# Six wider token blocks instead of eight in the first network of an attention and mixture-of-experts kernel

## The chip, the cores and the metric

The kernel runs on one core of one Trainium2 chip. The metric is the device time of one execution in microseconds. A core has TensorE (PE, the matrix multiplies; PEld is its weight load, which overlaps), VectorE (DVE), ScalarE (ACT), GpSimd (POOL) and SyncE (SP, which here only issues DMAs; ACT issues some too). Each engine executes its instructions in a fixed order and stops at the first whose inputs or buffers are not ready.

## The reference

The inputs are q, k, v (4 batches, 8 heads, 576 positions, 64 wide), the weights of a first gated network and those of a second, expert network. All products are done to nearly float32 precision.

```
scores = q @ k^T / 8, masked      # heads 0-3: the last 32 positions; heads 4-7: every 4th of the last 128
x   = softmax(scores) @ v                             # 2304 tokens x 512
xn  = x / sqrt(mean(x*x) + 1e-6) * rms_g
y   = (silu(xn @ w_gate) * (xn @ w_val)) @ w_out      # first network: 512 -> 1536 -> 512, weights in float64
P   = exp(y @ gate2 - max); 8 rounds of row and column normalisation, P *= 2304/8 in each
out = sum over 8 experts of P[:, e] * (relu(y @ w1[e]) @ w2[e])     # 512 -> 1024 -> 512
```

## The kernel before

Every value that a matrix multiply reads is split into a high and a low part of TensorE's reduced float32 format (tiles of `[128, 2, 512]`, slot 0 high, slot 1 low), and each product is done in three passes (high x high, high x low, low x high).

**Attention** goes by 20 tiles, five for each batch (four of 128 tokens and one of 64). A tile (`att_tile`, L148) is a chain: 32 or 16 small multiplies into `psS`; on DVE the mask is added into `sf` (tile `sc`), then maximum and subtraction (L191 to L200); Exp on ACT (L203); sums on DVE; four transposes into `psT` and a copy to `pt` (L219); the multiplies with v into `psX`; the division into `xf` (tile `xs`, L255); two Squares on ACT with a sum (L271); two small multiplies into `psR`; a power on POOL (L282); scaling on DVE (L284); four transposes into `psXT`; and the split into the columns of `xn` (L299, L300). The first five tiles use three sets of buffers (`Set`, L91): set 0 has its own K and V buffers `kbd` and `vbd`, sets 1 and 2 borrow six slots each of the weight pool `wx`. Tiles 5 to 19 all use set 0 in "rows" mode, one after the other: K and Q of the next tile are fetched by ACT's queue after the copy to `pt`, V after the Squares. `pt` and `xs` share one buffer (tag `px`), `q` and `sc` have one each, `psS` and `psX` share one pair of PSUM banks.

**First network.** The tokens are cut into eight blocks, per batch one of 256 (two tiles) and one of 320 (three tiles). For a block, 12 calls of `gemm_h` (L437) do 12 multiplies each into `pg` and `pv` (L447), as wide as the block, and then Silu on ACT, the product on DVE and the split of `h` on ACT and POOL. After each chunk of four such calls, `gemm_out` (L411) does 4 x 12 multiplies into `po` (L421) and adds them to `partial`; the last chunk writes `partial` to DRAM (`x2d`). A block thus takes 432 multiplies. Blocks 0 and 1 go chunk by chunk while the weights come in. From block 2 on, the attention of block i+1 is written ahead of the multiplies of block i, and a planner that simulates the engines fixes each engine's order, with the program's order as priority. `xn` has two buffers, one for even and one for odd blocks; `h` has five, `hf` two.

**Weights.** The 36 weight tiles of 128 x 512 float64 numbers are numbered in the order of their use. `split_double` (L314) takes each in two halves of 256 columns. A half takes an absolute value on ACT (L344), three operations on DVE (L345, L347, L350), a scaling on ACT (L354), an addition on POOL (L355), the high part on ACT for even numbers (L358) or on POOL for odd (L360), and the low part on DVE for the gate and value weights (L366) or POOL for the output weights (L364). Numbers 0 to 25 are loaded whole into a slot of `wx`, 26 to 35 by halves into a staging pool. The scratch `m` is one of three buffers of 256 columns for numbers below 12, and half a slot of `wx` from 12 to 25.

**Gate and second network.** `gate` (L517) reads 384 tokens of `x2d` at a time, six times in all, beside the multiplies of blocks 2 to 7 and the start of the second network. Towards the end of block 7, `tail` (L691) prepares the first inputs and weights of the second network (`x_load`, `x_split`, `moe2_weights`), whose tiles reuse the slots of the first network's weights as these come free. The second network's multiplies (L803, 384 columns; L860, 512 columns) fill the rest of the time.

Of the kernel before, what the change touches and what calls it, by code (L numbers as in the profile page):

```python
# [8 lines left out]
F32 = mybir.dt.float32  # L9
# [15 lines left out]
NEG = -1.0e30  # L25

# [6 lines left out]
def attention_moe_kernel(  # L33
# [57 lines left out]
    class Set:  # L91

        def __init__(self, first=None):
            self.work = None
            self.rows = False
            if first is None:
                self.q = None
                k = apool.tile([P, 2, 832], F32, name="kbd")  # L100
                self.k = [k[:, :, :320], k[:, :, 320:]]
                self.kload = [k]
                v = apool.tile([P, 2, 1024], F32, name="vbd")
                self.v = [v[:, :, :512], v[:, :, 512:]]
# [14 lines left out]
        def load_qk(self, n, queue=None):  # L119
            queue = queue or nc.sync  # L120
            b, t = divmod(n, 5)
            if self.work is None:
                self.q = apool.tile([P, 512], F32, tag="q", name=f"q_{n}", bufs=1)
            queue.dma_start(self.q, qt[b, t])
            for hh in range(2):
                c0 = 0
                for k in self.kload:
                    c1 = c0 + k.shape[2]
                    queue.dma_start(k[64 * hh : 64 * hh + 64, hh, :], kt_[b, t, hh, :, c0:c1])
                    c0 = c1  # L130

        def load_v(self, n, queue=None):
# [3 lines left out]
            for hh in range(2):  # L136
                for i, v in enumerate(self.vload):
                    queue.dma_start(v[64 * hh : 64 * hh + 64, hh, :], vt[b, t, hh, :, c * i : c * i + c])
# [9 lines left out]
    def att_tile(n, xn, c0, bufs, after_qk=None, after_pv=None):  # L148
# [14 lines left out]
        for hp in range(4):  # L163
            for g in range(4):
                off = hp * 160 + 32 * g if hp < 2 else ((hp - 2) * 4 + g) * 64
                if rows:
                    for s in range(2):
# [4 lines left out]
                            rhs=bufs.k[hp // 2][half, s, off : off + 64],  # L172
# [42 lines left out]
        if bufs.work is None:  # L215
            pt = apool.tile([P, 512], F32, tag="px", name=f"pt_{n}", bufs=1)
# [10 lines left out]
        for hp in range(4):  # L227
            vals = bufs.v[hp // 2].rearrange("p s (a g d) -> p s a g d", a=2, g=4)
            for g in range(4):
                if rows:  # L230
                    for s in range(2):
# [4 lines left out]
                            rhs=vals[half, s, hp % 2, g, :],  # L236
# [13 lines left out]
        if bufs.work is None:  # L250
            xf = apool.tile([P, 512], F32, tag="px", name=f"xs_{n}", bufs=1)
# [62 lines left out]
    def split_double(pool, src, name, gk, number, hi_eng, lo_eng):  # L314
# [701 lines left out]
```

## Time and profile before

| | us |
|---|---|
| three timed runs | 2147.39, 2156.18, 2156.72 |
| their median | 2156.18 |
| the profiled execution | 2151.64 |
| span of its trace, first to last instruction | 2149.9 |
| TensorE busy in the span | 2078.1 (97%) |
| VectorE, ScalarE, GpSimd busy | 1227.3, 893.7, 781.2 |

The profiled execution is 1.7 us longer than its span, and lies between the timed runs, 4.5 us under their median. A busy share is a mean over the whole span; the first 200 us, the next 390, the change to the second network (590 to 750) and the second network itself have different limits.

### The profile page before, as it was taken

To read this page: it belongs to the slowest core of one execution; us is meant where nothing else is said; L and a number is where in the kernel's file an instruction comes from. 1 tells how busy PE (TensorE), PEld (TensorE's weight loads), DVE (VectorE), ACT (ScalarE), POOL (GpSimd) and SP (SyncE) were. 2 spreads that over 40 slices of the span, in tenths; PEclk is the share of its full clock that TensorE was granted. 3 is DMA by queue.
4 is the path that set the end of the run, shared out by engine and by line. 5 is a ranking of instruction groups with operands and counts; after the bars stand their busy time and mean duration, and the time that the engine had idled before them with its cause. 6 is when DMAs were issued, how large, how long until landed. Compare 5 with 4: busy or idle time off the path is not lost.

```text
span 2149.9 us, 34621 instructions
## 1 busy us (share of the span) xinstructions
PE 2078.1 (97%) x13506; PEld 1900.2 (88%) x13506; DVE 1227.3 (57%) x2122; ACT 893.7 (42%) x1916; POOL 781.2 (36%) x853
## 2 busy tenths in 40 slices
PE   5788999999999999999999999999999999999999
PEld 4778999999988889899899988989998898999897
DVE  7987333324166756566655655665656466566553
ACT  5554443334245334434434443443344444334431
POOL 3765221212255424333413433433333333333420
PEclk7899999999999999999999999999999999999999
DMA  9323322212132212112212221221222122122110
GB/s 273 119 77 97 84 71 56 69 29 74 43 118 84 69 59 79 57 62 79 74 54 89 79 59 60 79 78 51 69 89 79 50 78 79 54 65 79 60 39 35
DMA packets 83397, 161.04 MB, mean 75 GB/s; under 512 B 10528, under 2 KB 18336, under 8 KB 83232
## 3 DMA queue, kind: packets, MB, share of 16 engines
q1 hardware_dynamic: 76128, 140.63, 21.4%
q10 hardware_dynamic: 7104, 18.19, 3.0%
q8 instruction: 106, 1.74, 0.3%
q14 instruction: 59, 0.48, 0.1%
HBM read 149.34 MB, written 9.44 MB: 74 GB/s over the span
## 4 chain that ended last, share of the span: by engine, by line
PE 85%; DVE 5%; ACT 3%; DMA 2%; POOL 2%; issue 2%; SPq 1%; ACTq 0%; POOLq 0%; DVEq 0%
PE py L860 36%; PE pa L803 18%; PE pb L803 9%; PE po L421 6%; PE pv L447 5%; PE pg L447 5%; PE pc L803 5%; DMA kbd<-in_kt 1%; PE psX L233 0%; PE psS L169 0%; DVE m_o L350 0%; DMA sd_g<-in_w_gate 0%; DMA vbd<-in_vt 0%; DVE m_o L345 0%; DMA st_w<-in_w 0%
## 5 line engine op out<-in xcount | busy, mean ns | idle before, releaser
L860 PE MATMUL py<-w,h 128*128 128x512 f32 x3456 | 860.9, 393 | 0.6 <-DVE acc L881 0.6
L860 PEld LDWEIGHTS py<-w,h 128*128 128x128 f32 x3456 | 644.0, 188 | 118.3 <-DVE acc L881 1.0
L597 POOL TENSOR_TENSOR w<-st_w,w 128x512 fp32r<-128x512 f32 x184 | 241.8, 1333 | 351.0 <-ACT w L596 343.8
L881 DVE SCALAR_TENSOR_TENSOR acc<-py,Pm,acc 128x512 f32<-128x512 f32 x264 | 194.3, 748 | 275.9 <-PE py L860 275.7
L803 PE MATMUL pa<-x_b,w 128*128 128x384 f32 x1152 | 254.3, 337 | 7.4 <-ACT w L579 6.5
L566 POOL TENSOR_TENSOR w1s<-w1r 128x256 f32<-128x256 f32 x92 | 75.0, 816 | 500.0 <-DVE w L580 499.0
L803 PE MATMUL pa<-x_t,w 128*128 128x384 f32 x1152 | 244.8, 337 | 0.0
L803 PEld LDWEIGHTS pa<-x_b,w 128*128 128x128 f32 x1152 | 207.1, 188 | 18.9 <-ACT w L579 7.7
L803 PEld LDWEIGHTS pa<-x_t,w 128*128 128x128 f32 x1152 | 206.9, 188 | 14.3 <-ACT pq L832 0.2
L447 PE MATMUL pv<-xn,w_v 128*128 128x320 f32 (+1 forms) x1152 | 185.1, 305 | 15.8 <-ACT hf L459 6.3
L421 PE MATMUL po<-h,w_o 128*128 128x320 f32 (+1 forms) x1152 | 179.3, 301 | 9.5 <-DVE partial L432 3.3
L596 ACT CAST w<-st_w 128x512 fp32r<-128x512 f32 x184 | 108.6, 621 | 190.9 <-PE pa L803 85.5
L447 PE MATMUL pg<-xn,w_g 128*128 128x320 f32 (+1 forms) x1152 | 182.6, 300 | 3.3 <-DVE hf L460 2.1
L447 PEld LDWEIGHTS pv<-xn,w_v 128*128 128x128 f32 x1152 | 165.6, 194 | 20.6 <-ACT hf L459 7.3
L421 PEld LDWEIGHTS po<-h,w_o 128*128 128x128 f32 x1152 | 161.9, 191 | 13.7 <-DVE partial L432 4.0
L447 PEld LDWEIGHTS pg<-xn,w_g 128*128 128x128 f32 x1152 | 164.1, 191 | 6.7 <-DVE hf L460 2.7
L462 POOL TENSOR_TENSOR h<-hf,h 128x256 fp32r<-128x256 f32 (+1 forms) x96 | 80.1, 837 | 218.1 <-ACT h L461 218.1
L580 DVE TENSOR_TENSOR w<-w1s,w 128x512 fp32r<-128x512 f32 x184 | 125.1, 705 | 22.0 <-ACT w L579 19.6
L580 DVE TENSOR_TENSOR w<-w1r,w 128x512 fp32r<-128x512 f32 x92 | 110.1, 1196 | 40.0 <-ACT w L579 39.4
L579 ACT CAST w<-w1s 128x512 fp32r<-128x512 f32 x184 | 110.9, 619 | 52.1 <-PE pc L803 17.0
L815 ACT ACTIVATE h<-pq 128x384 fp32r<-128x384 f32 x96 | 50.3, 524 | 185.6 <-DVE pq L844 185.5
L803 PE MATMUL pb<-x_t,w 128*128 128x384 f32 x576 | 125.2, 336 | 0.0
(160 smaller groups left out, 2697.3 us busy)
## 6 DMA issues: line engine op xcount, KB each, us to landing
st_w<-in_w SPq DMA_DIRECT2D x184, 256.0 KB, 2.8
w1r<-in_w SPq DMA_DIRECT2D x184, 256.0 KB, 2.9
vbd<-in_vt ACTq DMA_DIRECT2D x30, 256.0 KB, 4.0
kbd<-in_kt ACTq DMA_DIRECT2D x30, 208.0 KB, 3.5
sd_g<-in_w_gate SPq DMA_DIRECT2D x10, 512.0 KB, 6.9
sx<-x2d SPq DMA_DIRECT2D x24, 192.0 KB, 2.6
xr<-x2d SPq DMA_DIRECT2D x12, 384.0 KB, 3.7
out<-acc SPq DMA_DIRECT2D x18, 256.0 KB, 2.3
```

What stands on the lines that cost most here:

```text
L421: nc.tensor.matmul(po[:, :n], lhsT=ow[f][:, a, dc * P : dc * P + P], rhs=hs[blk, f][:, bb, :n], start=k == 0, stop=k == 11,)
L447: nc.tensor.matmul(ps[:, :n], lhsT=w[kt, fg][:, a, fo * P : fo * P + P], rhs=xn[:, kt, bb, :n], start=k == 0, stop=k == 11,)
L462: nc.gpsimd.tensor_tensor(out=h[:, 1, :n], in0=hf, in1=h[:, 0, :n].bitcast(F32), op=ALU.subtract)
L566: nc.gpsimd.tensor_tensor(out=s1, in0=a21, in1=a22f, op=ALU.add)
L579: nc.scalar.copy(hi, src)
L580: nc.vector.tensor_tensor(out=lo, in0=src, in1=hi.bitcast(F32), op=ALU.subtract)
L596: nc.scalar.copy(w[:, 0, :], st)
L597: nc.gpsimd.tensor_tensor(out=w[:, 1, :], in0=st, in1=w[:, 0, :].bitcast(F32), op=ALU.subtract)
L803: nc.tensor.matmul(ps[:, :TH], lhsT=w1s[ch, a, kt][:, s, q * P : q * P + P], rhs=xc[b, kt][:, t, :TH], start=first and k == 0, stop=k == 5 ...
L815: nc.scalar.activation(h[:, 0, :], src, AF.Relu)
L860: nc.tensor.matmul(ps, lhsT=hh[u, f, th][:, a, jj * P : jj * P + P], rhs=w2s[ch, f][:, bb, :], start=k == 0, stop=k == 11,)
L881: nc.vector.scalar_tensor_tensor(out=acc[j], in0=ps, scalar=Pm[:, tt, e : e + 1], in1=acc[j], op0=ALU.mult, op1=ALU.add)
```

## The change

Blocks become 256, 320, 384, 448, 448 and 448 tokens (2, 3, 3, 4, 4 and 4 tiles). `xn`, `h` and `hf` are sized for 448; `hf` has one buffer instead of two; `partial` has one buffer of 576 columns, whose two parts hold blocks 0 and 1. The gate reads 512, 384, 512, 384 and 512 tokens instead of six times 384. Set 0 borrows six slots of the weight pool `wr`; a new set `setn`, for tiles 5 to 19, has K and V buffers of half the size (the two heads on the two halves of the partitions, without a zero half). In it `pt` takes the buffer of `q`, and `xs` that of `sc`; K of the next tile is fetched after the copy to `pt`, Q and V after the Squares. Weights 4 to 31 are split 512 columns at a time, weights 0 to 31 are loaded whole and have their scratch in weight-pool slots, and 32 to 35 take staging and scratch from the same three staging buffers.

```diff
+BLK = 448
         def __init__(self, first=None):
-            self.rows = False
+            self.rows = first is None
             if first is None:
-                k = apool.tile([P, 2, 832], F32, name="kbd")
+                k = apool.tile([P, 832], F32, name="kall").unsqueeze(1)
...
-                v = apool.tile([P, 2, 1024], F32, name="vbd")
+                v = apool.tile([P, 1024], F32, name="vall").unsqueeze(1)
...
             else:
-                slots = [wx.tile([P, 2, 512], F32R, tag="w", name=f"first_{first}_{i}").bitcast(F32) for i in range(6)]
+                pool = wr if first == 0 else wx
+                slots = [pool.tile([P, 2, 512], F32R, tag="w", name=f"first_{first}_{i}").bitcast(F32) for i in range(6)]
...
+        def load_qv(self, n, queue):
+            self.load_q(n, queue)
+            self.load_v(n, queue)
...
-            pt = apool.tile([P, 512], F32, tag="px", name=f"pt_{n}", bufs=1)
+            pt = apool.tile([P, 512], F32, tag="q", name=f"pt_{n}", bufs=1)
...
-            xf = apool.tile([P, 512], F32, tag="px", name=f"xs_{n}", bufs=1)
+            xf = apool.tile([P, 512], F32, tag="sc", name=f"xs_{n}", bufs=1)
...
-        wide = number < 26
+        wide = number < 32
...
-            if number >= 12:
-                if number % 2 == 0:
-                    m_slot.append(wx.tile([P, 2, 512], F32R, tag="w", name=f"m_{name}").bitcast(F32))
-                scratch = m_slot[-1][:, number % 2, :].rearrange("p (j n) -> p j n", j=2)
-        for j in range(2):
-            cols = slice(256 * j, 256 * j + 256)
+            if number % 2 == 0:
+                m_pool = wr if number < 4 else wx
+                m_slot.append(m_pool.tile([P, 2, 512], F32R, tag="w", name=f"m_{name}").bitcast(F32))
+            scratch = m_slot[-1][:, number % 2, :]
+        step = 512 if wide and number >= 4 else 256
+        for j in range(0, 512, step):
+            cols = slice(j, j + step)
             if wide:
-                words = raw[:, 512 * j : 512 * j + 512]
+                words = raw[:, 2 * j : 2 * j + 2 * step]
             else:
-                pool_st, bufs = (stg, 3) if (2 * number + j) % 4 < 3 else (apool, 1)
-                words = pool_st.tile([P, 512], U32, tag="st", name=f"sd_{name}_{j}", bufs=bufs)
+                words = stg.tile([P, 512], U32, tag="st", name=f"sd_{name}_{j}", bufs=3)
...
-                mf = apool.tile([P, 256], F32, tag="m", name=f"m_{name}_{j}", bufs=3)
+                mf = stg.tile([P, 512], F32, tag="st", name=f"m_{name}_{j}", bufs=3)[:, :step]
...
-            partials[blk] = mpool.tile([P, 4, n], F32, tag=f"partial{blk % 2}", name=f"partial_{blk}", bufs=1)
+            if blk == 0:
+                both = mpool.tile([P, 4, 576], F32, tag="partial", name="partial_0", bufs=1)
+                partials[0], partials[1] = both[:, :, :256], both[:, :, 256:]
+            elif blk > 1:
+                partials[blk] = mpool.tile([P, 4, 576], F32, tag="partial", name=f"partial_{blk}", bufs=1)[:, :, :n]
...
-        hf = mpool.tile([P, 320], F32, tag="hf", name=f"hf_{blk}_{f}", bufs=2)[:, :n]
+        hf = mpool.tile([P, BLK], F32, tag="hf", name=f"hf_{blk}_{f}", bufs=1)[:, :n]
...
+    GATES = (0, 512, 896, 1408, 1792, NT)
...
-    for b in range(B):
-        blocks.append((b * S, 256, [(5 * b, 0), (5 * b + 1, 128)]))
-        blocks.append((b * S + 256, 320, [(5 * b + 2, 0), (5 * b + 3, 128), (5 * b + 4, 256)]))
+    for t0, t1 in ((0, 2), (2, 5), (5, 8), (8, 12), (12, 16), (16, 20)):
+        tok0 = starts[t0]
+        blocks.append((tok0, starts[t1] - tok0, [(t, starts[t] - tok0) for t in range(t0, t1)]))
...
             yield from att_tile(
-                tn, xns[i], c0, set0,
-                (lambda: set0.load_qk(tn + 1, nc.scalar)) if more else None,
-                (lambda: set0.load_v(tn + 1, nc.scalar)) if more else None,
+                tn, xns[i], c0, setn,
+                (lambda: setn.load_k(tn + 1, nc.scalar)) if more else None,
+                (lambda: setn.load_qv(tn + 1, nc.scalar)) if more else None,
...
-    ready = {2: (0,), 3: (1,), 4: (2,), 6: (3,)}
-    for i in range(2, 8):
-        if i < 7:
+    for i in range(2, 6):
+        if i < 5:
             run(block_att(i + 1))
-            spread(moe1_chunks([(i, 0), (i, 1), (i, 2)]), 34, [(later(g), 34) for g in ready.get(i, ())])
+            spread(moe1_chunks([(i, 0), (i, 1), (i, 2)]), 34, [(later(i - 2), 34)])
         else:
-            spread(moe1_chunks([(i, 0), (i, 1), (i, 2)]), 34, [(tail(), 34), (later(4), 34)])
+            spread(moe1_chunks([(i, 0), (i, 1), (i, 2)]), 34, [(tail(), 34), (later(3), 34)])
```

## Rows read from the trace of the kernel before

**Rows 1.** Busy time by stretch of the span. Columns: start and end, length, then busy us (instructions) of each engine, the granted TensorE clock as a share of full speed, DMA share and GB/s.

```profile
core 0: us, PE busy (x) PEld busy (x) DVE busy (x) ACT busy (x) POOL busy (x), PEclk, DMA share, GB/s
0.00:60.00 60.00, 32.74 (x412) 26.47 (x412) 45.22 (x121) 36.03 (x88) 24.23 (x38) 0.78 0.93 267
60.00:200.00 140.00, 118.05 (x994) 109.67 (x995) 124.47 (x268) 79.27 (x208) 101.31 (x137) 0.93 0.30 94
200.00:590.00 390.00, 385.23 (x4379) 375.84 (x4378) 123.65 (x283) 146.95 (x317) 84.43 (x103) 1.00 0.22 61
590.00:750.00 160.00, 146.63 (x789) 133.38 (x788) 108.65 (x206) 74.21 (x159) 85.06 (x85) 0.98 0.30 93
750.00:2149.00 1399.00, 1395.48 (x6938) 1254.82 (x6937) 825.29 (x1247) 557.22 (x1147) 486.12 (x492) 1.00 0.22 67
```

**Rows 2.** Twelve multiplies of one width in a row, from the chain of waits (start, us, what): block of 320 tokens, block of 256 tokens, second network at 512 columns.

```profile
341.64 1.76 PE pv L447 x12
407.72 1.44 PE pv L447 x12
734.49 8.29 PE py L860 x36
```

**Rows 3.** TensorE in order of time where only 384-column multiplies follow each other; the time of one is read from start to start.

```profile
641.43 2.24 PE L803 MATMUL pb<-x_t,w_a 128*128 128x384 f32 x12
643.51 1.20 PE L803 MATMUL pa<-x_t,w 128*128 128x384 f32 x6
644.55 2.24 PE L803 MATMUL pb<-x_t,w 128*128 128x384 f32 x12
```

**Rows 4.** VectorE in order of time, back to back operations of 256 and 512 columns.

```profile
53.64 0.68 DVE L262 TENSOR_TENSOR first<-psX,rs 128x512 f32<-128x512 f32 x1
54.24 0.19 DVE L209 RECIPROCAL rs<-sm 128x8 f32<-128x8 f32 x1
...
56.11 0.41 DVE L350 SCALAR_TENSOR_TENSOR m_g<-sd_g,m_g 128x256 uint32<-128x256 uint32 x1
56.44 0.28 DVE L345 TENSOR_SCALAR m_v<-m_v 128x256 f32<-128x256 f32 x1
```

**Rows 5.** GpSimd in order of time, back to back operations of 512 and 256 columns.

```profile
643.43 1.29 POOL L597 TENSOR_TENSOR w<-st_w,w 128x512 fp32r<-128x512 f32 x1 [1.61 <-ACT w L596]
644.68 0.74 POOL L566 TENSOR_TENSOR w1s<-w1r 128x256 f32<-128x256 f32 x1
645.38 1.06 POOL L568 TENSOR_TENSOR w1s<-w1r 128x256 f32<-128x256 f32 x1
```

**Rows 6.** The split's operations on VectorE, groups by line from 60 to 200 us (busy us, mean ns of one, idle before).

```profile
L350 DVE SCALAR_TENSOR_TENSOR m_o<-sd_o,m_o 128x256 uint32<-128x256 uint32 x24 | 16.1, 670 | 0.4
L347 DVE TENSOR_SCALAR m_o<-m_o 128x256 uint32<-128x256 uint32 x24 | 13.4, 560 | 0.4
```

**Rows 7.** The end of the weight split in the chain of waits.

```profile
194.67 0.72 DVE m_o L347
195.42 0.84 DVE m_o L350
196.32 0.73 POOL m_o L355
197.48 0.74 PE po L421 x4
```

**Rows 8.** TensorE in order of time, tiles 6 and 7 and the beginning of block 2 (its first multiplies are the `pg` of 256 columns at 210.27; `po` of 320 columns belongs to block 1).

```profile
146.88 0.33 PE L169 MATMUL psS<-kbd,q 64*32 64x64 f32 x12
...
190.59 0.60 PE L214 MATMUL psT<-cst,sc 128*128 128x128 f32 x4
...
207.34 0.60 PE L290 MATMUL psXT<-cst,xs 128*128 128x128 f32 x4
...
209.48 0.86 PE L169 MATMUL psS<-kbd,q 64*32 64x64 f32 x64
210.27 1.70 PE L447 MATMUL pg<-xn,w_g 128*128 128x256 f32 x12
...
220.38 0.86 PE L233 MATMUL psX<-vbd,pt 64*32 64x64 f32 x64
221.16 2.02 PE L421 MATMUL po<-h,w_o 128*128 128x320 f32 x12
...
226.45 0.86 PE L169 MATMUL psS<-kbd,q 64*32 64x64 f32 x64
...
229.53 0.63 PE L290 MATMUL psXT<-cst,xs 128*128 128x128 f32 x4
```

**Rows 9.** The same view later: the first multiplies of the tiles of one batch.

```profile
363.81 0.86 PE L169 MATMUL psS<-kbd,q 64*32 64x64 f32 x64
...
386.29 0.86 PE L169 MATMUL psS<-kbd,q 64*32 64x64 f32 x64
...
483.81 0.86 PE L169 MATMUL psS<-kbd,q 64*32 64x64 f32 x64
```

**Rows 10.** SP's queue at the start: DMA issues in order of time.

```profile
1.17 1.18 SPq L129 DMA_DIRECT2D kbd<-in_kt  x2
...
5.93 1.23 SPq L138 DMA_DIRECT2D vbd<-in_vt  x2
7.21 0.58 SPq L311 DMA_DIRECT2D sd_g<-in_w_gate  x1
```

**Rows 11.** TensorE's waits in the change to the second network.

```profile
634.52 1.40 PE L803 MATMUL pa<-x_b,w 128*128 128x384 f32 x6 [1.70 <-ACT w L579]
...
638.20 3.39 PE L803 MATMUL pa<-x_b,w 128*128 128x384 f32 x18 [1.20 <-ACT w L579]
...
650.49 1.32 PE L803 MATMUL pc<-x_b,w 128*128 128x384 f32 x6 [1.61 <-DVE h L816]
```

**Rows 12.** DMA issues: 512-column weights of the first network loaded by halves (count, KB each, median us to landing).

```profile
sd_o<-in_w_out SPq DMA_DIRECT2D x8, 256.0 KB, 2.6
```

More of the change, by code (lines that the diff above doesn't have):

```diff
@@ L120, in load_qk, with load_q @@
             queue = queue or nc.sync
+            self.load_q(n, queue)
+            self.load_k(n, queue)
+        def load_q(self, n, queue):
             b, t = divmod(n, 5)
@@ L124, in load_qk, with load_k @@
             queue.dma_start(self.q, qt[b, t])
+        def load_k(self, n, queue):
+            b, t = divmod(n, 5)
             for hh in range(2):
@@ L128, in load_qk @@
                     c1 = c0 + k.shape[2]
-                    queue.dma_start(k[64 * hh : 64 * hh + 64, hh, :], kt_[b, t, hh, :, c0:c1])
+                    queue.dma_start(k[64 * hh : 64 * hh + 64, 0 if self.rows else hh, :], kt_[b, t, hh, :, c0:c1])
                     c0 = c1
+        def load_qv(self, n, queue):
+            self.load_q(n, queue)
+            self.load_v(n, queue)
         def load_v(self, n, queue=None):
@@ L137, in load_v @@
                 for i, v in enumerate(self.vload):
-                    queue.dma_start(v[64 * hh : 64 * hh + 64, hh, :], vt[b, t, hh, :, c * i : c * i + c])
+                    queue.dma_start(v[64 * hh : 64 * hh + 64, 0 if self.rows else hh, :], vt[b, t, hh, :, c * i : c * i + c])
     def next_psum():
@@ L171, in att_tile @@
                             lhsT=qs[half, hp, g, :],
-                            rhs=bufs.k[hp // 2][half, s, off : off + 64],
+                            rhs=bufs.k[hp // 2][half, 0, off : off + 64],
                             start=True,
@@ L337, in split_double @@
             low, high = words[:, :, 0], words[:, :, 1]
[L338 to L339 removed]
+            hi, lo = w[:, 0, cols], w[:, 1, cols]
+            if wide:
+                mf = scratch[:, cols]
             else:
[L341 removed]
+                mf = stg.tile([P, 512], F32, tag="st", name=f"m_{name}_{j}", bufs=3)[:, :step]
             m = mf.bitcast(U32)
@@ L474, in moe1_chunks @@
             pending.append((blk, c))
-        if chunks[-1] == (7, 2):
+        if chunks[-1] == (5, 2):
             yield from gemm_out(*pending.pop())
@@ L521, in gate @@
         for kt in range(4):
-            st = stg.tile([P, 512], F32, tag="st", name=f"sx_{blk}_{kt}", bufs=3)[:, :TH]
-            nc.sync.dma_start(st, x2d[kt, :, TH * blk : TH * blk + TH])
-            hi, lo = (stg.tile([P, 512], F32R, tag="st", name=f"g{s}_{blk}_{kt}", bufs=3)[:, :TH] for s in range(2))
+            st = stg.tile([P, 512], F32, tag="st", name=f"sx_{blk}_{kt}", bufs=3)[:, :n]
+            nc.sync.dma_start(st, x2d[kt, :, t0:t1])
+            hi, lo = (stg.tile([P, 512], F32R, tag="st", name=f"g{s}_{blk}_{kt}", bufs=3)[:, :n] for s in range(2))
             nc.scalar.copy(hi, st)
@@ L599, in moe2_weights @@
             yield
-    set0 = Set()
-    set1, set2 = Set(1), Set(2)
+    set0, set1, set2 = Set(0), Set(1), Set(2)
+    setn = Set()
     set0.clear(nc.vector, nc.gpsimd)
@@ L622, in attention_moe_kernel, with rows_of @@
                     nc.sync.dma_start(cst[:, C_PM:C_G], consts[:, C_PM:C_G])
+    starts = [b * S + t * P for b in range(B) for t in range(5)] + [NT]
     blocks = []
-    for b in range(B):
-        blocks.append((b * S, 256, [(5 * b, 0), (5 * b + 1, 128)]))
-        blocks.append((b * S + 256, 320, [(5 * b + 2, 0), (5 * b + 3, 128), (5 * b + 4, 256)]))
+    for t0, t1 in ((0, 2), (2, 5), (5, 8), (8, 12), (12, 16), (16, 20)):
+        tok0 = starts[t0]
+        blocks.append((tok0, starts[t1] - tok0, [(t, starts[t] - tok0) for t in range(t0, t1)]))
     xns = {}
+    def rows_of(i):
+        return mpool.tile([P, 4, 2, BLK], F32R, tag="xn", name=f"xn_{i}", bufs=2)[:, :, :, : blocks[i][1]]
     def block_att(i):
         tok0, n, tl = blocks[i]
-        xns[i] = mpool.tile([P, 4, 2, n], F32R, tag=f"xn{i % 2}", name=f"xn_{i}", bufs=1)
+        xns[i] = rows_of(i)
         for tn, c0 in tl:
@@ L667, in second_att @@
     def second_att():
-        xns[1] = mpool.tile([P, 4, 2, 320], F32R, tag="xn1", name="xn_1", bufs=1)
+        xns[1] = rows_of(1)
         yield from together([
@@ L728, in attention_moe_kernel @@
     next_psum()
-    set0.rows = True
     run(block_att(2))
@@ L763, in side @@
     def side():
-        yield from gate(NT // TH - 1)
+        yield from gate(4)
         nc.vector.tensor_tensor(out=Pm, in0=L2[:, :, 0:8], in1=L2[:, :, 8:16], op=ALU.add)
```

23 lines of the change are left out of this document (11 added, 12 removed).

## The prediction

> **What bounds the kernel now.** I read the busy table by stretch first [rows 1], since the mean of 97% mixes four regimes. From 200 to 590 us, the first network from block 2 on, TensorE is busy for 385.2 of 390 us at full clock and VectorE for 124: there only fewer or shorter multiplies help. From 750 us the second network has TensorE busy for 1395.5 of 1399 us, and the change touches nothing in it. From 60 to 200 us VectorE is busy for 124.5 of 140 us and GpSimd for 101.3, TensorE for 118: the weights are being split, and TensorE waits. The end of that split stands in the chain of waits: the last three operations on an output weight run straight into a `po` multiply at 197.48 [rows 7]. From 590 to 750 us TensorE lacks 13.4 us. So four places can move: the split, the start of block 2 behind it, the 390 us of dense multiplies, and the change-over.
>
> Next I looked for what one multiply costs beyond its columns. Twelve of 320 columns take 1.76 us, 146.7 ns each; twelve of 256 take 1.44, 120.0 ns; 36 of 512 take 8.29, 230.3 ns [rows 2]; of 384, from start to start, 2.08 us for twelve, 173.3 ns [rows 3]. From 256 to 384 that is 0.417 ns a column and 13.3 ns a multiply; at 512 it is 17 ns. Fewer, wider multiplies over the same columns save this fixed part.
>
> **The wider blocks.** Blocks 0 and 1 keep their sizes. Blocks 2 to 7 take 3 x 432 x (146.7 + 120.0) ns = 345.6 us now. After, 432 at 384 columns and 1296 at 448. The trace has no 448: continuing the line of 320 and 384 gives 200.0 ns, the middle of 384 and 512 gives 201.8. The sum is 334.1 or 336.4 us; I take 200.9 ns and 335.2, a saving of 10.4 us (9.2 to 11.5), all of it on the path.
>
> One rule of the Trainium skill speaks against this. The page "TensorE: Matmul & The Clock Gate", section "Back-to-back issue gap", gives an isolated gap of N/2.4 + 2.5 ns; by it the 864 multiplies that go would be worth only 2.2 us, and my whole sum would be about 2149. Rows at four widths show five times that fixed part, so the rows go into the sum.
>
> `hf` has one buffer. After the last `pv` of a call come the product on VectorE (0.60 us at 512 columns [rows 4]), a copy on ScalarE (estimated alike) and GpSimd's low part (1.25 us [rows 5]): 2.5 us. The next `pg` ends 12 x 0.201 = 2.4 us after that `pv`, and its Silu is needed only another 2.4 us later, with the next `pv`. So the wait costs nothing where the engines are free; where they are full (before 200 us), ScalarE and VectorE queue split work behind it. I price it at 0 in the dense part and leave up to 5 us for the first part. `partial` with one buffer is written by block i+1 a whole chunk (28 us) after block i's last part went to DRAM: 0.
>
> **The split by 512.** Of the 28 weights that change, each loses three VectorE instructions, and 20 of them (gate and value) a fourth: 104. Back to back, a 256-column operation takes 0.33 us from start to start, one of 512 0.60 [rows 4]: a merged pair saves 0.06, together 6 us. On GpSimd 28 additions, 14 high and 8 low parts merge: 50 pairs at 2 x 0.70 - 1.25 = 0.15 us [rows 5], 7.5 us. If both lie on the path in turn, the split ends 13.7 us earlier; if only the longer one counts, or the coarser steps overlap less, it is nearer 5. The VectorE rows average 560 to 670 ns [rows 6] against 0.28 to 0.41 alone [rows 4], so these engines hold each other up, and a GpSimd step twice as long can hold VectorE twice as long. I take 5 us (bounds 0 and 13.7). Weights 32 to 35 now need two of three staging buffers for each half; the third lets the next half load meanwhile. At worst one load of 2.6 us [rows 12] shows per weight, 10 us; I take 0, because the chunk they serve comes last. Set 0 now loads K and V by 8 DMAs instead of 4: four issues of 0.6 us ahead of the gate weights [rows 10], 2.4 us at most. I count 1, against the earlier free scratch that numbers 4 to 11 gain.
>
> **Block 2 now needs a third tile.** Here the split's gain is at risk. Attention stands behind the split in the program's order: tile 6 had its scores at 146.88, and its softmax was transposed only at 190.59 [rows 8]. Its last transposes came at 207.34, and block 2 began at 210.27, as soon as that tile was there. Block 1 still had 48 `po` multiplies, 7 us, so its own work would have lasted to about 217. Tile 7 started at 209.48 and gave its last transposes at 229.53, 20 us later, when it was not yet wanted. After the change block 2 wants it. With a split shorter by 5 us TensorE runs out of old work near 212. If tile 7 follows tile 6 at the old distance it is there at 202.3 + 22.2 + 1.5 = 226; if lighter queues let it start while the split still runs, near 212. I take 219, halfway: against 217 now, 2 us lost, and the split's 5 us with them. Bounds: -14 (attention keeps up with the full gain of the split) and +14 (tile 7 at its present time, 231).
>
> The new buffers lengthen the tile chain. `xs` takes the buffer of `sc`, so the mask of tile n+1 waits for the last transposes of tile n; VectorE's multiplies for the dense part would queue behind it if the planner put it too early. Today tile 8's scores come at 226.45, 3.1 us ahead of tile 7's transposes at 229.53 [rows 8]; that lead goes. Q of the next tile is fetched after V's multiplies rather than before, and tile 8's scores came 6.1 us after tile 7's `psX` at 220.38, so the load has about that time. Tiles start 22.5 us apart (363.81, 386.29), and five take 120 us with their pause (363.81 to 483.81) [rows 9]. Four at 22.5 are 90 us; a 448 block offers 432 x 0.201 = 87 us and its own tiles' multiplies, about 3 us each, together 99; block 2 with 384 columns only 75 + 12 = 87. So block 3 is tight and blocks 4 and 5 are not. I price this at 0, with a bound of +13 for block 3 (a period of 25.6: 102 against 89).
>
> **The change-over.** The last chunks are 144 x 0.201 = 29 us long instead of 144 x 0.147 = 21, with the same preparation beside them. The three longest waits there sum to 4.5 us [rows 11]; I take 2 of them off (0 to 4.5).
>
> **Sum.** -10.4 (multiplies) + 2 (start of block 2, the split and the start inside it) - 2 (change-over) = -10.4. On the profiled execution's 2151.6 us this is 2141. That execution is 4.5 us under the median of the runs.
>
> **Rivals.**
> *Attention comes late* (slower). The place is the start of blocks 2 and 3. Tile 7 ends at its present time, +14, and block 3 waits another 13: 2151.6 - 10.4 + 14 + 13 - 2 = 2166. For it: tile 6 stood 44 us between scores and transposes in that stage. Against: the planner knows these waits and GpSimd and VectorE have less to do. It decides once tile 7's last transposes come after about 226.
> *Attention keeps up.* The split's 13.7 us count in full: 2151.6 - 10.4 - 13.7 - 2 = 2125.5. For it: the chain ran through the split until 197 [rows 7], and deeper scratch frees ScalarE. Against: the third tile.
> *The attention's pace replaces TensorE* as the bound in the dense part: what the multiplies save comes back as waits of TensorE for `xn`, 2151.6 + 2 - 2 = 2151. For it: 90 us of tiles against 87 in block 2. Against: five tiles have 120 us now and still pause.
> *Width saves little.* The fixed part grows from 13.3 ns at 384 columns to 17 at 512; if it were 20 ns at 448, the unseen width, the blocks would take 343 us and save 2: 2151.6 - 2 + 2 - 2 = 2149 to 2150. Against: 512 columns lie beyond 448 and have 17. The page's rule above would give the same time.
>
> **Chances.** The forecast (2131 to 2149) 0.47; late attention 0.18; attention keeping up 0.20; the pace as bound 0.13; no saving by width 0.02. A measurement can tell about 0.5% from no change, 10.8 us. Faster than 2140.8: half of the forecast's, nearly all of the second rival's, 0.46. Slower than 2162: most of the late case with the late staging buffers, 0.16. The rest, 0.38, lies between. The range reaches from below the keeping-up case's 2125.5 (2120) to just over the late one's 2166 (2168).
>
> **What would show it.** Twelve 448-column multiplies should take 2.40 to 2.42 us; the last `w_o` operation should end near 192, tile 7's `psXT` stand near 218, and the first 384-column `pg` close behind it. TensorE's idle time between there and the second network should stay under 8 us. A gap of over 10 us ahead of the first `pg` of block 2 or 3, ended by the split of `xn`, would make the late case right; a first `pg` of block 2 before 205 would make the second rival right; 448-column multiplies above 2.5 us a dozen would take the main term away.

## The result and the profile after

The changed kernel takes 2173.6 us (median of 4 runs, 2172.0 to 2177.5); the kernel before, in runs beside it, 2154.8. The ratio is 1.0096, 95% interval 1.0068 to 1.0124: about 1% slower, and above the predicted range. The profiled execution took 2172.0 us with a span of 2170.2, against 2149.9 before: 20.3 us to find.

Busy time by stretch of the changed kernel, the same stretches and columns as in [rows 1]:

```profile
core 0: us, PE busy (x) PEld busy (x) DVE busy (x) ACT busy (x) POOL busy (x), PEclk, DMA share, GB/s
0.00:60.00 60.00, 34.02 (x394) 25.25 (x394) 46.60 (x106) 30.34 (x62) 25.33 (x37) 0.91 0.79 248
60.00:200.00 140.00, 106.40 (x814) 98.41 (x814) 90.13 (x153) 63.81 (x129) 70.37 (x67) 0.82 0.28 86
200.00:590.00 390.00, 385.10 (x3682) 353.04 (x3683) 127.37 (x269) 145.81 (x284) 92.31 (x97) 0.99 0.24 64
590.00:750.00 160.00, 146.89 (x721) 131.66 (x720) 102.92 (x182) 71.52 (x147) 76.38 (x73) 0.96 0.29 93
750.00:2149.00 1399.00, 1397.92 (x6950) 1257.16 (x6951) 841.30 (x1263) 562.80 (x1157) 493.92 (x505) 1.00 0.21 66
```

The second line tells most. Before, VectorE was busy for 124.5 of these 140 us and TensorE for 118.1 at a clock of 0.93. Now every engine is less busy, TensorE does less at a clock of 0.82, and yet the stretch does not end sooner: the work runs past 200 us. An engine that bounded the stretch is relieved, and what bounds it now is no engine's busy time.

TensorE in order of time at the start of block 2 (compare [rows 8]; start, us, and in brackets the idle time before and what ended it):

```profile
229.37 0.60 PE L304 MATMUL psXT<-cst,xs 128*128 128x128 f32 x4
...
238.76 3.80 PE L439 MATMUL po<-h,w_o 128*128 128x320 f32 x24 [0.42 <-DVE partial L450]
...
244.61 0.85 PE L183 MATMUL psS<-kall,q 64*32 64x64 f32 x64 [1.72 <-issue]
245.39 0.66 PE L304 MATMUL psXT<-cst,xs 128*128 128x128 f32 x4
246.91 0.44 PE L465 MATMUL pg<-xn,w_g 128*128 128x384 f32 x1 [0.86 <-ACT xn L313]
```

Tile 6 gives its transposes at 229.4 (207.3 before), block 1's last `po` ends at 242.6, tile 7's transposes come at 245.4 and block 2 begins at 246.9. Before, old work would have lasted to 217.3 (210.27 and 48 `po` at 146.7 ns). So the start of block 2 lies **29.6 us later**. From there to the first `py` of the second network it is now 671.8 - 246.9 = 424.9 us, against 652.9 - 217.3 = 435.6: 10.7 less. From the first `py` to the end it is 1498.4 against 1497.0: 1.4 more. 29.6 - 10.7 + 1.4 = 20.3, the whole difference. The loss lies ahead of block 2.

### The profile page after: what moved, and what is told of

Same layout as the page of the kernel before. It is cut to its first block, busy times and chain, and to the rows that moved or that the text cites. A ratio compares the mean times of both kernels' runs of the same rounds, so it can differ in the third digit from the quotient of the medians.

```text
span 2170.2 us, 32476 instructions
## 1 busy us (share of the span) xinstructions
PE 2087.2 (96%) x12634; PEld 1879.2 (87%) x12634; DVE 1214.3 (56%) x1979; ACT 875.2 (40%) x1781; POOL 758.3 (35%) x777
## 4 chain that ended last, share of the span: by engine, by line
PE 86%; DVE 2%; issue 1%; ACT 1%; DMA 1%; POOL 0%; SPq 0%; ACTq 0%; DVEq 0%; POOLq 0%
PE py L884 36%; PE pa L827 18%; PE pb L827 9%; PE po L439 6%; PE pg L465 5%; PE pv L465 5%; PE pc L827 5%; PE psX L247 1%; PE psS L183 0%; DVE h L840 0%; PE pl L551 0%; PE psXT L304 0%; PE psT L228 0%; DVE w L602 0%; DVE x_t L531 0%
## 5 line engine op out<-in xcount | busy, mean ns | idle before, releaser
L827 PEld LDWEIGHTS pa<-x_t,w 128*128 128x128 f32 x1152 | 208.4, 189 | 14.8 <-ACT p L851 0.7
L465 PE MATMUL pv<-xn,w_v 128*128 128x448 f32 (+3 forms) x864 | 182.4, 353 | 17.8 <-ACT w_v L372 8.2
L465 PE MATMUL pg<-xn,w_g 128*128 128x448 f32 (+3 forms) x864 | 179.7, 351 | 7.0 <-DVE hf L478 6.1
L465 PEld LDWEIGHTS pv<-xn,w_v 128*128 128x128 f32 x864 | 152.3, 198 | 31.2 <-ACT w_v L372 9.3
L439 PE MATMUL po<-h,w_o 128*128 128x448 f32 (+3 forms) x864 | 172.9, 345 | 1.9 <-DVE partial L450 1.0
L465 PEld LDWEIGHTS pg<-xn,w_g 128*128 128x128 f32 x864 | 152.2, 197 | 17.4 <-DVE hf L478 7.1
L439 PEld LDWEIGHTS po<-h,w_o 128*128 128x128 f32 x864 | 146.4, 190 | 12.2 <-DVE partial L450 2.0
L480 POOL TENSOR_TENSOR h<-hf,h 128x448 fp32r<-128x448 f32 (+3 forms) x72 | 75.9, 1054 | 211.4 <-ACT h L479 207.0
L601 ACT CAST w<-w1s 128x512 fp32r<-128x512 f32 x184 | 111.3, 620 | 54.1 <-PE pc L827 17.9
## 6 DMA issues: line engine op xcount, KB each, us to landing
kall<-in_kt ACTq DMA_DIRECT2D x30, 208.0 KB, 3.3
```

What stands on the lines that cost most here:

```text
L439: nc.tensor.matmul(po[:, :n], lhsT=ow[f][:, a, dc * P : dc * P + P], rhs=hs[blk, f][:, bb, :n], start=k == 0, stop=k == 11,)
L465: nc.tensor.matmul(ps[:, :n], lhsT=w[kt, fg][:, a, fo * P : fo * P + P], rhs=xn[:, kt, bb, :n], start=k == 0, stop=k == 11,)
L480: nc.gpsimd.tensor_tensor(out=h[:, 1, :n], in0=hf, in1=h[:, 0, :n].bitcast(F32), op=ALU.subtract)
L601: nc.scalar.copy(hi, src)
L827: nc.tensor.matmul(ps[:, :TH], lhsT=w1s[ch, a, kt][:, s, q * P : q * P + P], rhs=xc[b, kt][:, t, :TH], start=first and k == 0, stop=k == 5 ...
```

## The experiments

All compare with the kernel before. Times and ratios were taken beside it on the same chip; the places in the table come from one trace of each kernel, taken on several chips, against the trace of [rows 1]. The table has the end of the last low part of a value weight and of an output weight (the end of the split), the first `pg` of block 2, the first `py`, and the span, in us. In kernels whose block 2 has two tiles, block 1's last 44 to 48 `po` run beside it. To compare such a kernel with one of three tiles, they are added to its start of block 2 at 146.7 ns each: 217.3 stands for the 210.3 of before.

Second traces of two kernels show how far a place moves by chance: after_step256 again has block 2 at 238.1 and its first `py` at 664.4, mix384 again 230.1 and 654.9. So differences of 1 to 3 us between places mean nothing here, and single times differ by more: the kernel before took from 2146.8 to 2157.9 us.

| kernel | value split ends | output split ends | block 2 | first `py` | span |
|---|---|---|---|---|---|
| before | 180.4 | 199.2 | 210.3 | 652.9 | 2149.9 |
| after | 198.9 | 223.6 | 246.9 | 671.8 | 2170.2 |
| after_step256 | 187.4 | 213.5 | 236.1 | 661.5 | 2160.5 |
| before_step512 | 184.2 | 202.2 | 211.9 | 652.9 | 2151.9 |
| before_scratch4 | 189.7 | 208.2 | 217.6 | 656.6 | 2154.2 |
| after256_attfirst | 194.8 | 220.8 | 245.3 | 670.7 | 2171.5 |
| before_staging3 | 179.8 | 208.0 | 213.5 | 652.2 | 2150.8 |
| before_hf1 | 175.3 | 193.1 | 208.4 | 656.6 | 2156.2 |
| after_blocks8 | 200.2 | 224.8 | 233.7 | 685.3 | 2184.6 |
| after256_blocks7 | 188.9 | 214.7 | 222.8 | 660.7 | 2160.0 |
| mix384 | 181.0 | 200.7 | 229.2 | 656.1 | 2155.4 |
| mix_blocks8 | 180.9 | 200.5 | 212.1 | 652.5 | 2153.5 |

**The 512-column step undone.**

```diff
-        step = 512 if wide and number >= 4 else 256
+        step = 256
```

> The changed kernel with every weight split 256 columns at a time, all else kept. Coarse-step theory (a 512-column step makes each weight a serial chain over three engines, 4.5 to 7 us each, where two halves used to overlap): the last low part of a value weight comes back from 197.7 to about 180 us, the first multiply of block 2 from 246.9 to about 228, the time from 2173 to about 2155. One-hf-buffer theory and slots theory (Silu waiting for GpSimd at the head of ScalarE's queue, or loads waiting for weight-pool slots): both stay within 4 us of the changed kernel, 2170 to 2176.

> The changed kernel with every weight split 256 columns at a time again, timed. One look gave 2162.3 us. Theory: the split by 512 columns is about half of the whole loss, so the ratio to the kernel before is 1.004 to 1.007, against 1.0096 for the changed kernel. Rival: the recovery of one look was chance; the ratio is 1.008 or more.

A single run had a span 9.7 us shorter than after's; timed, the ratio is 1.0066 (1.0053 to 1.0079) against 1.0096 for the changed kernel, which is 6.5 us. The two intervals overlap a little, but block 2 begins 10.8 us earlier, 8.8 in the second trace, well over the scatter. So the step costs 6 to 10 us, a third to a half of the loss. That is about half of what the theory expected (a value split at 180, block 2 at 228, 2155 us), and more than the two other theories allow. How the step costs time, the trace of the changed kernel shows. All engines in order of time, one value weight:

```profile
178.59 0.65 ACT L359 ACTIVATE m_v<-sd_v 128x512 f32<-128x512 f32 x1
...
179.28 0.43 DVE L360 TENSOR_SCALAR m_v<-m_v 128x512 f32<-128x512 f32 x1 [1.10 <-ACT m_v L359]
179.74 0.43 DVE L362 TENSOR_SCALAR m_v<-m_v 128x512 uint32<-128x512 uint32 x1
180.20 0.69 DVE L365 SCALAR_TENSOR_TENSOR m_v<-sd_v,m_v 128x512 uint32<-128x512 uint32 x1
181.03 1.28 POOL L370 TENSOR_TENSOR m_v<-m_v,sd_v 128x512 uint32<-128x512 uint32 x1 [4.04 <-DVE m_v L365]
...
182.34 0.72 ACT L372 ACTIVATE w_v<-m_v,cst 128x512 fp32r<-128x512 f32 x1 [2.54 <-POOL m_v L370]
...
183.09 0.75 DVE L380 SCALAR_TENSOR_TENSOR w_v<-m_v,cst,w_v 128x512 fp32r<-128x512 f32 x1 [2.20 <-ACT w_v L372]
183.11 0.79 PE L465 MATMUL pv<-xn,w_v 128*128 128x256 f32 x2 [4.89 <-ACT w_v L372]
...
183.76 0.42 DVE L360 TENSOR_SCALAR m_v<-m_v 128x512 f32<-128x512 f32 x1
```

A weight is one chain: three operations on VectorE, the addition on GpSimd, the high part on ScalarE, the low part on VectorE. The next weight's chain begins on VectorE at 183.76, 4.48 us after this one's at 179.28. VectorE works 0.43 + 0.43 + 0.69 + 0.75 = 2.3 us of that, and waits 2.20 us in the middle; TensorE waits 4.89. At 256 columns VectorE fills that hole with the other half. VectorE in order of time in after_step256:

```profile
179.54 0.86 DVE L380 SCALAR_TENSOR_TENSOR w_v<-m_v,cst,w_v 128x256 fp32r<-128x256 f32 x1 [0.29 <-ACT w_v L372]
180.70 0.48 DVE L380 SCALAR_TENSOR_TENSOR w_v<-m_v,cst,w_v 128x256 fp32r<-128x256 f32 x1 [0.29 <-ACT w_v L372]
181.10 0.28 DVE L360 TENSOR_SCALAR m_v<-m_v 128x256 f32<-128x256 f32 x1
181.42 0.29 DVE L362 TENSOR_SCALAR m_v<-m_v 128x256 uint32<-128x256 uint32 x1
181.68 0.29 DVE L360 TENSOR_SCALAR m_v<-m_v 128x256 f32<-128x256 f32 x1
181.89 0.42 DVE L365 SCALAR_TENSOR_TENSOR m_v<-sd_v,m_v 128x256 uint32<-128x256 uint32 x1
```

The waits ahead of the low part are 0.29 us instead of 2.20; the two halves pass through one behind the other. Over the whole stretch from 60 to 200 us the groups by line (busy us, mean ns, idle before) have 14.6 + 8.6 = 23.2 us of such waits in the changed kernel (first two lines), and 7.2 in after_step256:

```profile
L380 DVE SCALAR_TENSOR_TENSOR w_v<-m_v,cst,w_v 128x512 fp32r<-128x512 f32 x9 | 8.2, 912 | 14.6 <-ACT w_v L372 8.5 <-POOL w_v L374 6.1
L380 DVE SCALAR_TENSOR_TENSOR w_g<-m_g,cst,w_g 128x512 fp32r<-128x512 f32 x8 | 7.4, 927 | 8.6 <-ACT w_g L372 4.6 <-POOL w_g L374 4.0
...
L380 DVE SCALAR_TENSOR_TENSOR w_g<-m_g,cst,w_g 128x256 fp32r<-128x256 f32 x16 | 11.7, 741 | 3.6 <-POOL w_g L374 2.0 <-ACT w_g L372 1.5
L380 DVE SCALAR_TENSOR_TENSOR w_v<-m_v,cst,w_v 128x256 fp32r<-128x256 f32 x20 | 11.6, 591 | 3.6 <-POOL w_v L374 2.7 <-ACT w_v L372 0.9
```

A wait is not yet a loss. Over the last four value weights, one of which is shown above, both kernels go at about the same pace, and the lag of the changed kernel stays near 12 us. It arose before them: the low parts of the first value weight of the middle chunk end at 111.3 against 109.0 us, those of its last at 132.4 against 126.4, and those of the last chunk's gate weights at 156.6 to 177.8 against 148.4 to 166.1.

**The step alone, in the kernel before** (weights 12 to 25, the ones with scratch of their own; `wide` still ends at 26):

```diff
...
-        for j in range(2):
-            cols = slice(256 * j, 256 * j + 256)
...
+        step = 512 if wide and number >= 12 else 256
+        for j in range(512 // step):
+            cols = slice(step * j, step * j + step)
...
```

> The kernel before with weights 12 to 25 (those with scratch in weight-pool slots) split 512 columns at a time, all else kept. Coarse-step theory: 14 of the 28 weights, so about half of the loss of the split, the last low part of a value weight 5 to 12 us later than 179.7 and the time 2157 to 2165. Fewer instructions alone, as I had priced them: 3 us earlier, 2148. The hf and slots theories expect no loss here, 2146 to 2153.

The value split ends 3.8 us later, block 2 begins 1.6 later, the span is 2.0 longer: the sign of after_step256, for half as many weights, but less than the 5 to 12 us and the 2157 us or more that the theory expected. Only the split's delay is over the scatter; the rest can't be told from no change by a single run.

**Scratch in the weight slots.** In the kernel before, weights 4 to 11 take their scratch from the slots too, as in the change:

```diff
-            if number >= 12:
+            if number >= 4:
...
-            if wide and number >= 12:
+            if wide and number >= 4:
```

> The kernel before, with the scratch of weights 4 to 11 too in weight-pool slots instead of the three small buffers. Deep-scratch theory (with room for more weights in flight, the planner splits weights 4 to 11 ahead of the second group of tiles, tiles 2 to 4, whose last transposes then come near 80 us instead of 67, and weights 13 and on wait for the pool slots that those tiles hold): last transposes of tile 4 after 75 us, block 2 at least 4 us later than 210, time 2155 to 2165. Without it: 2147 to 2153, tile 4 within 4 us of 67.

TensorE in order of time, the transposes of tiles 2 to 4 in before_scratch4 (before, they begin at 63.3, 64.8 to 66.1 and 67.0):

```profile
76.19 0.60 PE L290 MATMUL psXT<-cst,xs 128*128 128x128 f32 x4
78.06 0.41 PE L290 MATMUL psXT<-cst,first 128*128 128x128 f32 x2 [1.27 <-DVE first L284]
...
86.16 1.09 PE L290 MATMUL psXT<-cst,first 128*128 128x128 f32 x4 [3.68 <-DVE first L284]
```

With free scratch the planner puts more splits ahead of these tiles; in the changed kernel the tiles come at 77.0 and 82.6 likewise. Both splits end 9 us later and block 2 begins 7.3 later, as expected. The span is 4.3 longer, the time 2156.0 against 2152.6 beside it, too little to be told by a single run. The next run put the tiles first again, in the changed kernel with the 256-column step:

```diff
-            with behind(("sub", 4), ("exp", 4)):
+            with behind(("lo", 4), ("hi", 4)):
```

> The changed kernel split by 256, with weights 8 to 11 queued behind the last step of tile 4 instead of its softmax. Deep-scratch theory: tile 4's last transposes move from 84 to 70 or earlier, weight 13 starts before 78 instead of 84, and block 2 starts 5 to 12 us earlier than 236: 2150 to 2156. If the slots are not what holds weight 13: no gain, 2158 to 2166.

The tiles came back (66.6 to 70.4), but the weights held back were simply late: weight 13 began at 94 us instead of 83, the value split ended 7.4 us after that of after_step256, and the span was 11.0 longer. So the scratch delays the split and block 2, as before_scratch4 shows, but that late tiles are the way in which it does was not confirmed; it stays open.

**Three staging buffers for weights 32 to 35**, words and scratch alike, in the kernel before:

```diff
-                pool_st, bufs = (stg, 3) if (2 * number + j) % 4 < 3 else (apool, 1)
+                pool_st, bufs = (stg, 3) if number >= 32 or (2 * number + j) % 4 < 3 else (apool, 1)
...
-                mf = apool.tile([P, 256], F32, tag="m", name=f"m_{name}_{j}", bufs=3)
+                m_pool, wm, bm = (stg, 512, "st") if number >= 32 else (apool, 256, "m")
+                mf = m_pool.tile([P, wm], F32, tag=bm, name=f"m_{name}_{j}", bufs=3)[:, :256]
```

> The kernel before with one edit: the last four weights (32 to 35) take both their words and their scratch from the three shared staging buffers, as in the changed kernel. Before, their splits begin at 178, 181, 190 and 193 us and the last low part of an output weight ends at 199.2; in the changed kernel with the 256-column step they begin 8 us apart. Theory: two of three buffers per half leave no load ahead, so a weight costs 7 to 9 us instead of 4 to 5, the last output weight ends at 205 to 214 us and, as the chunk it serves is the last of the old work, block 1's last po multiply ends 4 to 10 us later than 223.2; block 2 can fill that, so the span is 2152 to 2158 us (ratio 1.001 to 1.004). Rival, as the prediction had it: the loads stay hidden, the last output weight ends within 2 us of 199.2 and the span within 2 us of 2149.9.

ScalarE in order of time, the first operations on the last halves:

```profile
192.64 0.43 ACT L345 ACTIVATE m_o<-sd_o 128x256 f32<-128x256 f32 x1 [0.26 <-DMA sd_o<-in_w_out]
...
196.75 0.43 ACT L345 ACTIVATE m_o<-sd_o 128x256 f32<-128x256 f32 x1 [0.81 <-DMA sd_o<-in_w_out]
...
200.50 0.44 ACT L345 ACTIVATE m_o<-sd_o 128x256 f32<-128x256 f32 x1 [0.81 <-DMA sd_o<-in_w_out]
...
203.37 0.43 ACT L345 ACTIVATE m_o<-sd_o 128x256 f32<-128x256 f32 x1 [0.98 <-DMA sd_o<-in_w_out]
```

Halves stand some 4 us apart and wait for their DMA, and the output split ends 8.8 us later. The split's delay came as expected, the loss of time (1.001 to 1.004) did not: the ratio is 0.9998 (0.9985 to 1.0011). Block 2's multiplies, ready at 213.5, 3.2 us later than before, fill the gap. In the changed kernel block 2 is not ready, and this cover is missing; what the buffers cost there alone was not measured.

**The third tile of block 2.** First the changed kernel (256-column step) with two tiles in block 2 and wider blocks later. Here and below, the loop over the blocks and the places of the gate's sections follow the list:

```diff
-    for t0, t1 in ((0, 2), (2, 5), (5, 8), (8, 12), (12, 16), (16, 20)):
+    for t0, t1 in ((0, 2), (2, 5), (5, 7), (7, 10), (10, 13), (13, 17), (17, 20)):
```

> The changed kernel split by 256, with blocks of 256, 320, 256, 320, 384, 448 and 320 tokens, so that block 2 has two tiles again. Third-tile theory: block 2's first multiply comes at 222 to 226 instead of 236, and after the 5 us that the narrower blocks cost the time is 2155 to 2159. If block 2 waits for the split and the old work alone: 2164 to 2168.

Block 2 begins 13.3 us earlier than in after_step256, but 44 `po` of block 1, 6.5 us, then run beside it, so the tile's own part is 6.9 us. The span is 2160.0 instead of 2160.5 and the time 2161.8, where 2155 to 2159 was expected: with the split still late, the tile decided nothing. Some 3 of the 6.9 us are tile 7's own multiplies, which only move, and the blocks after it are narrower. Then the opposite: mix384 has the split, scratch, staging and two `hf` of the kernel before, with the changed kernel's attention buffers, single `partial` and gate sections, and three tiles in block 2; mix_blocks8 differs from it in the list of blocks alone, which is the old one:

```diff
-    for t0, t1 in ((0, 2), (2, 5), (5, 8), (8, 11), (11, 14), (14, 17), (17, 20)):
+    for t0, t1 in ((0, 2), (2, 5), (5, 7), (7, 10), (10, 12), (12, 15), (15, 17), (17, 20)):
```

> The changed kernel's buffers for attention, with the split, scratch and staging of before (steps of 256, three small scratch buffers), two hf buffers, and blocks of 256, 320, 384, 320, 384, 320, 320 tokens. If the split's scratch, staging and steps are the loss, the split ends near 180 as before and only block 2's third tile is left: block 2 starts at 220 to 228 and the time is 2142 to 2152. If the attention buffers are the loss: over 2156.

> mix384 again, timed against the kernel before. One look gave 2157.2 us, 1.0021 of the kernel before beside it. If the third tile takes back what five wider blocks save (5.8 us), the ratio is 0.999 to 1.003, no change that can be told; the rival, that these attention buffers with blocks of 384 are a gain hidden by one look, wants under 0.997.

> The split, scratch, staging, hf buffers and the list of eight blocks (256, 320, four times) of the kernel before, with the changed kernel's attention buffers and gate sections alone. Theory: what is left of the loss in mix384 at the start of block 2 (229.2 us against 217 of old work before) is the third tile, not the attention buffers. Then the first pg of block 2 stands at 209 to 214 us, right behind tile 6, the dense stretch costs its old 345.6 us against 339.8 in mix384 (5.8 more), and the span is 2146 to 2153 us, a ratio of 0.998 to 1.001. Rival: the attention buffers themselves (xs in the place of sc, Q fetched later, pt in the place of q) slow the tiles: tile 7's psXT and the waits in the dense stretch stay as in mix384 or worse, and the span is 2157 to 2165 us.

Timed, mix384 is at 1.0027 (1.0017 to 1.0037) and mix_blocks8 at 1.0024 (1.0015 to 1.0033): both a little slower than the kernel before, and no difference between them. The single run of mix384, 2157.2 us, lay above the expected 2142 to 2152, where its rival had put a loss by the attention buffers. mix_blocks8 tests that. TensorE in order of time in mix384:

```profile
208.59 0.60 PE L304 MATMUL psXT<-cst,xs 128*128 128x128 f32 x4
...
217.11 3.79 PE L440 MATMUL po<-h,w_o 128*128 128x320 f32 x24
223.23 0.85 PE L183 MATMUL psS<-kall,q 64*32 64x64 f32 x64 [1.72 <-DMA q<-in_qt]
227.62 1.09 PE L304 MATMUL psXT<-cst,xs 128*128 128x128 f32 x4 [3.54 <-DVE xs L298]
229.17 0.69 PE L466 MATMUL pg<-xn,w_g 128*128 128x384 f32 x1 [0.46 <-ACT xn L313]
```

With the split at its old pace (181.0) old work ends at 220.9 and TensorE waits for tile 7 until 229.2. In mix_blocks8, same buffers but two tiles, block 2 begins at 212.1; with block 1's 48 `po` that is 219.1. So the third tile costs about 10 us where the split is in time. The stretch from there to the first `py`, 426.9 us instead of 433.4, gives back 6.5: some 3 since tile 7's own multiplies are done by then, and about 2.8 by wider multiplies (the rate of 384 columns is read below). mix_blocks8 reaches its first `py` at 652.5, as before, so its 3.6 us of span lie behind that: from 650 to 750 us TensorE is busy for 88.5 us instead of 92.4. That cost of the buffers or the gate sections was not expected (0.998 to 1.001), and which of them it is stays open.

**One `hf` buffer** in the kernel before, and the old list of **eight blocks** in the changed kernel:

```diff
-        hf = mpool.tile([P, 320], F32, tag="hf", name=f"hf_{blk}_{f}", bufs=2)[:, :n]
+        hf = mpool.tile([P, 320], F32, tag="hf", name=f"hf_{blk}_{f}", bufs=1)[:, :n]
```

> The kernel before with one hf buffer instead of two, all else kept. One-hf-buffer theory: the split ends at least 8 us later and the time is over 2160. Coarse-step theory: within 4 us of before, 2148 to 2156.

```diff
-    for t0, t1 in ((0, 2), (2, 5), (5, 8), (8, 12), (12, 16), (16, 20)):
+    for t0, t1 in ((0, 2), (2, 5), (5, 7), (7, 10), (10, 12), (12, 15), (15, 17), (17, 20)):
```

> The changed kernel with the old eight blocks of 256 and 320, all else kept (buffers stay sized for 448). Third-tile theory (block 2 waits for a third tile): the first multiply of block 2 comes at least 10 us earlier than 246.9. Coarse-step, hf and slots theories: the split still ends near 198 us, block 2 starts within 5 us of the end of the old work (about 242), and the time is 2173 plus the 5 us that the wider multiplies saved, 2175 to 2180.

With blocks of 256 and 320 and one `hf`, the single run is 6.3 us longer in span, nearly all of it between block 2's start and the first `py` (448.2 against 442.6). The theory that this buffer delays the split (8 us or more) fails: the value split ends 5.1 us earlier. TensorE's waits from 250 to 600 us in before_hf1 (us in total, times, longest), where the kernel before has 2.8 us in the same line:

```profile
PE pv L447 <- ACT hf L459: 4.5, 5, 1.6
```

All of TensorE's waits there sum to 6.6 us, against those 2.8; the rest was not traced. The changed kernel has no such line there: with its wide blocks the chain is covered. Eight blocks on its buffers, where the line is back with 2.3 us, are 14.4 us slower than its six, more than the 2175 to 2180 us that any theory had. Block 2 begins 13.2 us earlier there, 6.2 when its 48 `po` are counted. So on these buffers the wider blocks are a gain.

## Why the prediction was wrong

**The failed step is the start of block 2**, priced at +2, measured at +29.6 against an allowed -14 to +14. Under it three terms failed.

*The split by 512* was counted as 5 us gained, bounds 0 and 13.7. It costs 10.8 us at the start of block 2 (246.9 against 236.1; 8.8 by the second trace). The sum of saved instructions was right in sign: VectorE and GpSimd are less busy. But that sum was taken for time on the path, although the chain of waits in [rows 7] passes through VectorE, GpSimd and TensorE in turn. The text even said that a GpSimd step twice as long can hold VectorE twice as long, and still excluded a loss without a reason.

*The earlier free scratch* was counted as a gain that pays 1 us of DMA issues; before_scratch4 shows 7.3 us lost at block 2.

*Staging for weights 32 to 35* was priced at 0 because their chunk comes last. In the kernel before that holds (0.9998), though the split ends 8.8 us later; block 2's multiplies cover it there, and the same change takes that cover away. What it costs in the changed kernel was not measured.

*The third tile* was seen as the risk, and tile 7 put at 218. It came at 245.4, mostly since tile 6 was late by 22 us. What the tile itself costs at block 2 is shown by the three pairs of kernels that differ in the list of blocks alone, with the `po` beside block 2 counted: 6.2 us in the changed kernel (240.7 against 246.9), 6.9 with the step of 256 (229.2 against 236.1), 10.1 with the old split (219.1 against 229.2). Late old work covers part of the wait.

So of the 29.6 us the step has 10.8 and the tile 6.9, and 11.9 are left (229.2 against 217.3). Scratch 7.3, staging 3.2 and the attention buffers 1.8 (212.1 against 210.3) would make 12.3, but each is from a kernel of its own and places scatter by 1 to 3 us; that sum was not shown in one kernel. The chain is longer as predicted: tile 7's mask on VectorE starts at 230.01, right behind tile 6's transposes, whose `xs` has its buffer.

**The second term that failed is the multiplies, -10.4, measured at about -3.6.** TensorE in order of time in the changed kernel:

```profile
318.65 2.28 PE L465 MATMUL pg<-xn,w_g 128*128 128x384 f32 x12
320.77 2.28 PE L465 MATMUL pv<-xn,w_v 128*128 128x384 f32 x12
322.89 0.51 PE L439 MATMUL po<-h,w_o 128*128 128x384 f32 x2
...
584.96 2.62 PE L439 MATMUL po<-h,w_o 128*128 128x448 f32 x12
587.42 0.51 PE L551 MATMUL pl<-g,wg 128*16 128x384 f32 x2
...
589.00 2.62 PE L465 MATMUL pg<-xn,w_g 128*128 128x448 f32 x12
591.46 2.62 PE L439 MATMUL po<-h,w_o 128*128 128x448 f32 x12
593.92 0.51 PE L551 MATMUL pl<-g,wg 128*16 128x384 f32 x2
```

From start to start, twelve of 448 columns take 2.46 us, 205 ns each, not 200.9, and twelve of 384 take 2.12 us, 176.7 ns each: the 173.3 was read in the second network, and the first network does not reach it. With 432 at 176.7 and 1296 at 205 the blocks cost 342.0 us, 3.6 saved, a third of the term. Fewer multiplies save a fixed part each, as predicted, but that part grows with the width, from 13.3 ns at 320 columns to 16.7 and 18.3, and eats most of the gain. The sign that was to take the main term away, over 2.5 us a dozen at 448, did not show it.

That the stretch came out 10.7 shorter is a coincidence: tile 7's multiplies, some 3 us, now lie ahead of it, and TensorE's waits from 250 to 600 us sum to 1.1 us instead of 2.8. The rest of it was not traced.

**Right at about 0:** `hf` at the wide widths, `partial`, and the tiles' pace. Block 3's tiles follow 24 us apart (269, 293, 317), later ones up to 26.5, and TensorE is busy for 339.5 of the 340 us from 250 on, so block 3 did not wait. **The change-over**, -2, gave nothing. TensorE's waits there, against three that sum to 4.5 us in [rows 11]:

```profile
651.68 1.65 PE L827 MATMUL pa<-x_b,w 128*128 128x384 f32 x4 [4.88 <-ACT w L601]
...
668.85 1.33 PE L827 MATMUL pc<-x_b,w 128*128 128x384 f32 x6 [0.97 <-DVE h L840]
```

They sum to 5.9. With the short waits for `partial` and `h` at the end of the last block, which shrink from 1.7 to 0.3, both kernels have 6.2 us.

**The rivals.** Late attention had the sign and 2166 us, but its test, a gap of over 10 us ahead of block 2, did not come: TensorE had old work until 242.6. The case that happened, a split that gets slower, was not among them. *Width saves little* had 0.02, with 20 ns beyond the columns at 448; 18.3 was measured, so as to the multiplies this rival was nearer than the forecast. Its counterargument, that 512 columns have 17 ns, held for another network.

Two of the prediction's figures do not follow from its own: half of 0.47 and nearly all of 0.20 make 0.43 at most, not 0.46, and block 3's bound of +13 sets 102 us against 89, where the same paragraph has 87. Nothing here rests on them.

## What to carry to other kernels

Where a tile of data passes through several engines in turn, price a coarser step by the period of the chain, not by the busy time that it saves: ask which other tile fills each engine's wait, and whether it still fits. A cost priced at nothing because other work covers it must be checked against the whole change, since another edit may take that cover away. And the first block after a preparing stage should need as little as possible: with the old split, a third tile there cost 10 us, and the wider blocks behind it gave back about 3. Lastly, read the cost of an instruction where it will run: the same width took 173.3 ns in one network and 176.7 in the other.

## What the hardware showed that was not expected

Counting 0.417 ns for a column (26.7 ns for the 64 from 256 to 320), a multiply of the first network has 13.3 ns beyond its columns at 256 and 320 [rows 2], 16.7 at 384 and 18.3 at 448. By the column that is 0.469 ns, then 0.458, 0.460 and 0.458: beyond 320 columns width saved nothing there. In the second network it is 13.3 ns at 384 and 17 at 512 [rows 2, 3], 0.451 and 0.450 by the column. Why the two networks differ is open. The rule in the Trainium skill, "TensorE: Matmul & The Clock Gate", section "Back-to-back issue gap", gives an isolated multiply N/2.4 + 2.5 ns, by estimate 189 at 448; the measured 205 decides.

After a stretch in which TensorE waited, it also ran at a lower clock. In the changed kernel, the last stretches before block 2:

```profile
180.00:200.00 20.00, 9.41 (x36) 7.73 (x36) 11.46 (x22) 6.59 (x13) 7.92 (x9) 0.65 0.18 61
200.00:215.00 15.00, 14.70 (x93) 14.69 (x94) 7.09 (x19) 7.51 (x21) 9.82 (x15) 0.79 0.22 66
```

After 9.4 busy us in 20, it is busy for 14.7 of the next 15 us at a granted clock of 0.79, part of the time at 1.2 GHz instead of 2.4; before, the clock there was 1.00. That makes up to 15 x 0.21 = 3 us of the late start, an estimate from these rows.
